# Delta-rule attention before two MoE layers: Gram tiles split by ScalarE and GpSimd, the unit diagonal by an identity product, block inverses spread with a full mask, norms of several groups at once

## The chip, the cores and the metric

One core of a Trainium2 chip. The metric is the device time of one execution, in microseconds, here as the median of three runs. Engines in the text: TensorE (PE, with PEld for its weight loads), VectorE (DVE), ScalarE (ACT), GpSimd (POOL) and SyncE (SP, which issues most DMAs).

## What is computed

The attention is a delta rule: per batch and head a 48x48 state is read and corrected at each of 768 steps. Two mixture-of-experts layers follow; the first is dense here, the second routes each token to one of eight experts.

```python
# q, k, v: [4, 8, 768, 48]; beta: [4, 8, 768]
k_n = k / (np.linalg.norm(k, axis=-1, keepdims=True) + 1e-06)
for t in range(S):
    y[:, :, t] = einsum('bhd,bhde->bhe', q[:, :, t], state)
    v_old = einsum('bhde,bhd->bhe', state, kt)
    state = state + bt * einsum('bhd,bhe->bhde', kt, vt - v_old)
x = y as [3072, 384]
x = leaky_relu(x @ w_in) @ w_out                 # d_ff 2048
out = x + gate * (relu(x @ w1[e]) @ w2[e])       # e: argmax of 8, only where x @ w_skip > 0
```

## The kernel before

The 768 steps are cut into six chunks of 128, the four batches into two pairs: twelve groups `i`, each one chunk of two batches of eight heads. Numbers are kept as a pair of f16 tiles, high and low part, so most products are two or three matmuls.

For a group, stage by stage: `prep` splits k and q into f16 parts and writes them to DRAM; `load_k`, `load_q` fetch them in the layouts that the products need. `norms` (L171) takes the squared norms of 128 tokens and 16 batch-heads on ScalarE and VectorE, an inverse square root by three Newton steps, and leaves four scales in the tile `dd`. `gram` (L221) is called four times per batch (`x` = 0 for k with k, `x` = 1 for k with q; `q` = 0, 1 for four heads each): 8 to 12 matmuls into PSUM, four ScalarE scalings into `g32` (L244), a GpSimd select that keeps the strict upper triangle (L245), for `x` = 0 past the first group a second one that writes 1 on the diagonal (L248), then VectorE makes the high part `gh` (L251) and the low part `gl` (L252). The buffers `g32` are two in rotation. The first group (`("hl", 0) in k`) gets its diagonal later, on the f16 tile, at L893.

`image` writes `gh` to DRAM, `sub16` reads its 16x16 diagonal blocks back and inverts them on VectorE (L273, L275), and `blocks` (L285) reads these inverses as `zc` and spreads them into block-diagonal 128x128 tiles `z128` on VectorE and `x128` on GpSimd (both L296), by a product with the mask `m8`, which is [128, 8] and repeated over the innermost 16 elements. `inv` builds the inverse of the whole triangle from the blocks: `pp` (L313) needs `x128`, `px` (L320), `pz` (L326); between rounds L329 restores the identity in parts of the tile `pe` on GpSimd, from the f32 identity. `solve` (L347) takes the chunk through: `ks`, `u0`, a first residual `r1` with `gh` and `gl`, `d1`, a second residual `r2`, `d2`, the state update `su` and the output `y`. `product` (L362) issues the matmuls of one of them, eight heads with 48 columns each.

The first MoE layer of a group (`m_up`, `m_down`, L753 to L785) starts when its group's `solve` is done and fills TensorE between the attention's products. Its two weight matrices are narrowed from 64-bit patterns by three VectorE operations per tile (L579 to L581), 32 tiles, early in the run: no `inv` but the first before 24 are in, no `solve` but the first before all 32 are. The second MoE layer follows after the attention.

The order of emission is written out by hand in `start()` for the first group and its loads; then a planner (`emit`) runs the stages as threads, with gates between them and due times from the table `T`. The tile framework orders each engine's instructions by a simulated timeline and by the priorities given there. Engines run their own instructions in order, so one that waits holds those behind it. Neither `T` nor the gates change.

Of the kernel before, what the change touches and what calls it, by code (L numbers as in the profile page):

```python
# [48 lines left out]
class Attention:  # L49
# [4 lines left out]
    def __init__(self, ctx, tc, kq, ktok, vtok, bet, ident):  # L54
# [15 lines left out]
        def mask(n, step, end, start):  # L70
# [13 lines left out]
        self.m8 = cp.tile([128, 8], F16, name="m_8")  # L84
        nc.vector.memset(self.m8, 1.0)
        nc.gpsimd.affine_select(out=self.m8, in_=self.m8, pattern=[[-16, 8]], compare_op=ALU.is_ge, fill=0.0,
                                base=0, channel_multiplier=1)
        nc.gpsimd.affine_select(out=self.m8, in_=self.m8, pattern=[[16, 8]], compare_op=ALU.is_ge, fill=0.0,
                                base=15, channel_multiplier=-1)
        self.pe = [cp.tile([128, H, C], F16, name=f"pe{i}") for i in range(2)]  # L90
# [80 lines left out]
    def norms(self, c, b0):  # L171
        nc = self.nc
        kt = self.ktile(c, b0)
        N = 2 * H
        be = self.p1.tile([128, N], F32, tag="be", name="be")
        nc.sync.dma_start(out=be, in_=self.bet[c * C:(c + 1) * C, b0 * H:(b0 + 2) * H])
# [3 lines left out]
        small = lambda nm: self.p1.tile([128, N], F32, tag=nm, name=nm)  # L180
        ss, y, t, nrm, d = (small(x) for x in ("ss", "y0", "t1", "nrm", "dd"))
        nc.vector.tensor_reduce(out=ss, in_=sq.rearrange("p b (h d) -> p (b h) d", d=D), axis=AX.X, op=ALU.add)
# [9 lines left out]
        nc.vector.tensor_scalar_add(out=nrm, in0=t, scalar1=1e-6)  # L192
        nc.vector.tensor_tensor(out=d, in0=nrm, in1=nrm, op=ALU.mult)
        nc.vector.reciprocal(out=d, in_=d)
        nc.vector.tensor_tensor(out=d, in0=d, in1=be, op=ALU.mult)
        dd = self.p4.tile([128, 4, N], F32, tag="d4", name="d4")
        for x, (src, f) in enumerate(((d, 2.0 ** -16), (d, 2.0 ** -8), (d, 256.0), (nrm, 256.0))):
            self.last = (nc.gpsimd if c + b0 else nc.vector).tensor_scalar(out=dd[:, x], in0=src, scalar1=f, scalar2=None, op0=ALU.mult)
        for j in range(2):
            self.tk[c, b0 + j]["dd"] = dd[:, :, j * H:(j + 1) * H]  # L200
# [20 lines left out]
    def gram(self, c, b, x, q, tag="g"):  # L221
# [63 lines left out]
    def blocks(self, c, b0):  # L285
# [6 lines left out]
        for j in range(2):  # L292
            k = self.tk[c, b0 + j]
            for x, nm in enumerate(("z128", "x128")):
                t = k[nm] = (self.p4 if x == 0 else self.p2).tile([128, H, C], F16, tag=nm, name=nm)
                (nc.gpsimd if x else nc.vector).tensor_tensor(out=t.rearrange("p h (g w) -> p h g w", w=16),  # L296
                                        in0=zc[:, x, j * H:(j + 1) * H].unsqueeze(2).to_broadcast([128, H, 8, 16]),
                                        in1=self.m8.unsqueeze(1).unsqueeze(3).to_broadcast([128, H, 8, 16]), op=ALU.mult)

    def inv(self, c, b):  # L300
# [7 lines left out]
        for n, m in ((16, self.m16), (32, self.m32)):  # L308
# [16 lines left out]
            for h in range(H):  # L325
# [3 lines left out]
            nc.gpsimd.tensor_copy(out=pe.rearrange("p h (g w) -> p h g w", w=64)[:, :, :, ws],  # L329
                                  in_=self.ident.rearrange("p (g w) -> p g w", w=64)[:, :, ws].unsqueeze(1).to_broadcast([128, H, 2, 16]))  # L330
# [16 lines left out]
    def solve(self, c, b):  # L347
# [14 lines left out]
        def product(nm, terms):  # L362
# [978 lines left out]
```

## Time and profile before

| | |
|---|---|
| median of 3 runs | 1164.93 us (1161.44 to 1170.25) |
| the profiled execution | 1159.18 us, of which its span is 1157.4 us |
| TensorE busy | 891.7 us, 77% |
| VectorE busy | 819.5 us, 71% |
| ScalarE busy | 617.4 us, 53% |
| GpSimd busy | 530.1 us, 46% |

Three stretches: to about 214 us the start, with the weight narrowing and the first group; to about 864 us the other eleven groups of attention with the first MoE layer in between; from there the last part of the first MoE layer and the second. The page's chain of waits covers only the last few microseconds before the end, so the stretches are read by the busy time of each engine in them and by what TensorE waited for. Busy time counts an instruction from its start to its end on the engine, also where it is held up on the way; overlapped matmuls count once.

### The profile page before, as it was taken

How to read it: one execution, taken by the hardware profiler on the slowest of the kernel's cores; microseconds unless marked ns; L12 is line 12 of the kernel's file. 1: busy time of each engine (PE TensorE's matmuls, PEld its weight loads, DVE VectorE, ACT ScalarE, POOL GpSimd, SP SyncE). 2: the span in 40 equal slices, each digit the busy share in tenths (PEclk: the TensorE clock that was granted, in tenths of full speed). 3: DMA queues.
4: the chain of work that ended last, by engine and by line, in shares of the span. 5: the costliest groups of instructions: out<-in, count | busy, mean ns of one | idle time of the engine just before them, and what ended most of it. 6: DMA issues, size and time to landing. Idle time of an engine off the chain costs nothing. (4 is left out here: it accounts for less than half of the span.)

```text
span 1157.4 us, 26616 instructions
## 1 busy us (share of the span) xinstructions
PE 891.7 (77%) x10164; PEld 680.7 (59%) x10164; DVE 819.5 (71%) x1814; ACT 617.4 (53%) x1406; POOL 530.1 (46%) x575
## 2 busy tenths in 40 slices
PE   2056778278886987778788979979987949998995
PEld 1056556265764766557566757667766637675763
DVE  6999998495986787566878575593447737777761
ACT  4476666255754755456355637464526425565540
POOL 4575685375455447364466544443224114332111
PEclk9999987678988898989989998999887979998998
DMA  7834775444454444354443212120108447788740
GB/s 206 227 89 135 226 181 124 83 141 85 127 96 105 110 103 107 37 124 76 126 106 66 70 21 70 25 65 15 43 28 230 127 144 256 258 281 265 234 149 16
DMA packets 201618, 144.03 MB, mean 124 GB/s; under 512 B 115070, under 2 KB 183892, under 8 KB 201482
## 3 DMA queue, kind: packets, MB, share of 16 engines
q1 hardware_dynamic: 189168, 123.24, 40.8%
q10 hardware_dynamic: 8570, 10.76, 3.3%
q0 software_dynamic: 3744, 8.27, 2.2%
q8 instruction: 81, 1.33, 0.5%
q14 instruction: 55, 0.45, 0.2%
HBM read 111.91 MB, written 30.92 MB: 123 GB/s over the span
## 5 line engine op out<-in xcount | busy, mean ns | idle before, releaser
L771 POOL TENSOR_TENSOR gll<-gg,ghh 128x512 f16<-128x512 f32 x96 | 119.0, 1242 | 99.1 <-ACT ghh L769 89.1
L761 PEld LDWEIGHTS <-wih 128*128 128x128 f16 x1152 | 118.9, 107 | 41.8 <-issue 18.1
L784 PE MATMUL o<-wol,ghh 128*128 128x394 f16 (+2 forms) x416 | 132.9, 325 | 8.0 <-DVE wol L608 8.0
L783 PE MATMUL o<-woh,ghh 128*128 128x394 f16 (+2 forms) x416 | 132.7, 329 | 4.7 <-ACT ghh L769 4.7
L244 ACT ACTIVATE g<-g,d 128x128 f32<-128x128 f32 x384 | 110.4, 376 | 41.4 <-DVE gl L252 23.8
L785 PE MATMUL o<-woh,gll 128*128 128x394 f16 (+2 forms) x416 | 124.3, 329 | 6.5 <-POOL gll L771 6.4
L761 PE MATMUL ph<-xh,wih 128*128 128x256 f16 x576 | 109.2, 302 | 12.8 <-ACT gg L766 10.6
L767 DVE SCALAR_TENSOR_TENSOR gg<-gg 128x512 f32<-128x512 f32 x96 | 83.4, 869 | 43.7 <-ACT gg L766 43.6
L761 PE MATMUL ph<-xl,wih 128*128 128x256 f16 x576 | 108.1, 299 | 2.3 <-DVE xl L691 2.3
L761 PE MATMUL ph<-xh,wil 128*128 128x256 f16 x576 | 108.2, 296 | 0.0
L245 POOL TENSOR_SCALAR_AFFINE_SELECT g<-g 128x512 f32<-128x512 f32 x96 | 72.8, 758 | 77.1 <-ACT g L244 67.6
L769 ACT CAST ghh<-gg 128x512 f16<-128x512 f32 x96 | 59.8, 623 | 83.3 <-DVE gg L767 83.0
L766 ACT COPY gg<-ph 128x512 f32<-128x512 f32 x96 | 56.4, 587 | 62.0 <-PE ph L761 52.4
L251 DVE CAST gh<-g 128x512 f16<-128x512 f32 x96 | 66.6, 696 | 30.0 <-POOL g L245 26.5
L1208 POOL DMA_INDIRECT out_dram<-y,ix x24 | 27.1, 1131 | 118.2 <-DVE y L1206 105.7
L252 DVE TENSOR_TENSOR gl<-g,gh 128x512 f16<-128x512 f32 x96 | 80.2, 836 | 0.7
L428 DVE SCALAR_TENSOR_TENSOR w1l<-ws,w1h 128x768 f16<-128x768 f32 x60 | 59.0, 996 | 27.6 <-ACT w1h L427 25.7
L273 DVE TENSOR_TENSOR tmp<-bt,z 128x15 f32<-128x15 f16 (+4 forms) x180 | 56.8, 316 | 29.5 <-DMA bt<-ai 19.6
L427 ACT ACTIVATE w1h<-ws 128x768 f16<-128x768 f32 x60 | 49.8, 840 | 39.0 <-DMA ws<-in_moe_w_dram 24.6
L296 POOL TENSOR_TENSOR x<-zc,m 128x1024 f16<-128x1024 f16 x24 | 56.5, 2372 | 29.3 <-DMA zc<-im 29.3
L1177 PEld LDWEIGHTS <-w1h 128*128 128x128 f16 x720 | 58.4, 99 | 19.2 <-issue 7.7
L747 POOL DMA_INDIRECT lst<-ids_i,pi x24 | 27.3, 1138 | 89.8 <-DMA lst<-ids_i,pi 45.6
(267 smaller groups left out, 2743.3 us busy)
## 6 DMA issues: line engine op xcount, KB each, us to landing
ws<-in_moe_w_dram SPq DMA_DIRECT2D x120, 384.0 KB
kt<-in_ktok_dram SPq DMA_DIRECT2D x24, 384.0 KB
x<-in_kq_dram SPq DMA_DIRECT2D x22, 384.0 KB
sc<-hl SPq DMA_DIRECT2D x22, 384.0 KB
raw<-in_moe_w_out_dram ACTq DMA_DIRECT2D x16, 384.0 KB
ai<-gh SPq DMA_DIRECT2D x24, 256.0 KB
x2s<-xs SPq DMA_DIRECT2D x24, 192.5 KB
vs<-in_vtok_dram SPq DMA_DIRECT2D x24, 192.0 KB
```

What stands on the lines that cost most here:

```text
L244: nc.scalar.activation(out=g32[:, j], in_=g[:, j], func=AF.Copy, scale=k["dd"][:, x, h:h + 1])
L245: nc.gpsimd.affine_select(out=g32, in_=g32, pattern=[[0, 4], [1, C]], compare_op=ALU.is_gt, fill=0.0, base=0, channel_multiplier=-1)
L251: self.last = nc.vector.tensor_copy(out=gh[:, hs], in_=g32)
L252: nc.vector.tensor_tensor(out=gl[:, hs], in0=g32, in1=gh[:, hs], op=ALU.subtract)
L428: nc.vector.scalar_tensor_tensor(out=lo, in0=src, scalar=scale, in1=hi, op0=ALU.mult, op1=ALU.subtract)
L761: nc.tensor.matmul(ph[:, j], lhsT=wt[:, d, fs], rhs=xx[:, d], start=(n == 0), stop=(n == 3 * KD - 1))
L767: nc.vector.scalar_tensor_tensor(out=g, in0=g, scalar=0.01, in1=g, op0=ALU.mult, op1=ALU.max)
L769: nc.scalar.copy(out=gh, in_=g)
L771: nc.gpsimd.tensor_tensor(out=gl, in0=g, in1=gh, op=ALU.subtract)
L783: nc.tensor.matmul(o, lhsT=gh[:, j, ts], rhs=wo[0][:, f, cols], start=(f == 0), stop=False)
L784: nc.tensor.matmul(o, lhsT=gh[:, j, ts], rhs=wo[1][:, f, cols], start=False, stop=False)
L785: nc.tensor.matmul(o, lhsT=gl[:, j, ts], rhs=wo[0][:, f, cols], start=False, stop=(f == NF1 - 1))
```

## The change

Five edits. (1) In `gram`, for all but the first group, the high part is a ScalarE copy and the low part a GpSimd subtraction; VectorE made both. The second select is gone, and L893 too. (2) `solve` gets the unit diagonal by one more matmul, of a 128x128 f16 identity with all eight heads at once (384 columns), ahead of `r1` and of `r2`. (3) `m8` is [128, 8, 16], so that the mask is read with unit step, and `x128` is made on VectorE like `z128`. (4) L329 runs on VectorE, from the f16 identity. (5) `norms` takes several groups: 0 and 1 alone, 2 and 3 together, 4 to 7, 8 to 11; loads, squares and reductions stay one per group, the chain of small operations after them is run once for all. Its `be` load now comes ahead of the first `kt` load.

```diff
-        self.m8 = cp.tile([128, 8], F16, name="m_8")
+        self.m8 = cp.tile([128, 8, 16], F16, name="m_8")
...
+        self.id16 = cp.tile([128, 128], F16, name="id16")
+        nc.vector.tensor_copy(out=self.id16, in_=ident)
...
-    def norms(self, c, b0):
+    def norms(self, groups):
         nc = self.nc
-        kt = self.ktile(c, b0)
-        N = 2 * H
...
-        yield 0, T["nl"]
-        sq = self.pl.tile([128, 2, HD], F32, tag="ld", name="sq")
-        nc.scalar.activation(out=sq, in_=kt, func=AF.Square)
...
+        n, (c0, b0) = len(groups), groups[0]
+        N = 2 * H * n
+        small = lambda nm: self.p1.tile([128, 8 * H], F32, tag=nm, name=nm)[:, 0:N]
...
+        for i, (c, b) in enumerate(groups):
+            kt = self.ktile(c, b)
+            yield 0, T["nl"]
+            sq = self.pl.tile([128, 2, HD], F32, tag="ld", name="sq")
+            nc.scalar.activation(out=sq, in_=kt, func=AF.Square)
+            nc.vector.tensor_reduce(out=ss[:, 2 * H * i:2 * H * (i + 1)], in_=sq.rearrange("p b (h d) -> p (b h) d", d=D),
+                                    axis=AX.X, op=ALU.add)
...
-        if x == 0 and not ("hl", 0) in k:
-            nc.gpsimd.affine_select(out=g32, in_=g32, pattern=[[0, 4], [1, C]], compare_op=ALU.not_equal,
-                                    fill=1.0, base=0, channel_multiplier=-1)
         hs = slice(4 * q, 4 * q + 4)
-        self.last = nc.vector.tensor_copy(out=gh[:, hs], in_=g32)
-        nc.vector.tensor_tensor(out=gl[:, hs], in0=g32, in1=gh[:, hs], op=ALU.subtract)
+        if ("hl", 0) in k:
+            self.last = nc.vector.tensor_copy(out=gh[:, hs], in_=g32)
+            nc.vector.tensor_tensor(out=gl[:, hs], in0=g32, in1=gh[:, hs], op=ALU.subtract)
+        else:
+            nc.scalar.copy(out=gh[:, hs], in_=g32)
+            nc.gpsimd.tensor_tensor(out=gl[:, hs], in0=g32, in1=gh[:, hs], op=ALU.subtract)
...
-                (nc.gpsimd if x else nc.vector).tensor_tensor(out=t.rearrange("p h (g w) -> p h g w", w=16),
+                nc.vector.tensor_tensor(out=t.rearrange("p h (g w) -> p h g w", w=16),
                                         in0=zc[:, x, j * H:(j + 1) * H].unsqueeze(2).to_broadcast([128, H, 8, 16]),
-                                        in1=self.m8.unsqueeze(1).unsqueeze(3).to_broadcast([128, H, 8, 16]), op=ALU.mult)
+                                        in1=self.m8.unsqueeze(1).to_broadcast([128, H, 8, 16]), op=ALU.mult)
...
-            nc.gpsimd.tensor_copy(out=pe.rearrange("p h (g w) -> p h g w", w=64)[:, :, :, ws],
-                                  in_=self.ident.rearrange("p (g w) -> p g w", w=64)[:, :, ws].unsqueeze(1).to_broadcast([128, H, 2, 16]))
+            nc.vector.tensor_copy(out=pe.rearrange("p h (g w) -> p h g w", w=64)[:, :, :, ws],
+                                  in_=self.id16.rearrange("p (g w) -> p g w", w=64)[:, :, ws].unsqueeze(1).to_broadcast([128, H, 2, 16]))
...
-        def product(nm, terms):
+        def product(nm, terms, plus=None):
             p = self.ps.tile([128, H, D], F32, tag=f"s{b % 2}", name=nm)
+            if plus is not None:
+                nc.tensor.matmul(p, lhsT=self.id16, rhs=plus, start=True, stop=False)
...
-        p = product("r1", [(of(ah), uh), (of(al), uh)])
+        p = product("r1", [(of(ah), uh), (of(al), uh)], uh)
...
-        p = product("r2", [(of(ah), ul)])
+        p = product("r2", [(of(ah), ul)], ul)
...
+    together = {0: 1, 1: 1, 2: 2, 4: 4, 8: 4}
+
     def stage_n(i):
-        c, p = groups[i]
-        yield from att.norms(c, 2 * p)
+        if i in together:
+            yield from att.norms([(c, 2 * p) for c, p in groups[i:i + together[i]]])
...
-        for b in range(2):
-            g = att.tk[0, b]["g", 0][0]
-            nc.gpsimd.affine_select(out=g, in_=g, pattern=[[0, H], [1, C]], compare_op=ALU.not_equal,
-                                    fill=1.0, base=0, channel_multiplier=-1)
```

## Rows read from the trace of the kernel before

**Rows 1.** Profile page: the span, and busy time of each engine

```profile
span 1157.4 us, 26616 instructions
...
PE 891.7 (77%) x10164; PEld 680.7 (59%) x10164; DVE 819.5 (71%) x1814; ACT 617.4 (53%) x1406; POOL 530.1 (46%) x575
```

**Rows 2.** Busy time of each engine in two stretches (stretch, its length, then by engine)

```profile
core 0: us, PE busy (x) PEld busy (x) DVE busy (x) ACT busy (x) POOL busy (x), PEclk, DMA share, GB/s
40.00:200.00 160.00, 106.62 (x1075) 86.25 (x1075) 150.08 (x313) 100.50 (x265) 108.53 (x113) 0.91 0.58 156
214.00:864.00 650.00, 525.09 (x6776) 404.44 (x6776) 441.53 (x1040) 348.37 (x853) 326.05 (x364) 0.90 0.35 80
```

**Rows 3.** Waits of TensorE, 214 to 864 us: total, times, longest

```profile
PE pp L313 <- POOL x L296: 41.9, 15, 16.8
PE y L366 <- DVE gh L251: 15.9, 7, 5.4
PE pz L326 <- DVE x L322: 12.2, 8, 3.9
PE d L366 <- ACT r L388: 9.5, 2, 7.3
PE ph L761 <- ACT gg L766: 6.4, 5, 3.1
```

**Rows 4.** VectorE's groups of instructions, 0 to 215 us: busy, mean ns of one

```profile
L252 DVE TENSOR_TENSOR gl<-g,gh 128x512 f16<-128x512 f32 x26 | 20.8, 803 | 0.0
...
L251 DVE CAST gh<-g 128x512 f16<-128x512 f32 x26 | 17.0, 660 | 1.7 <-POOL g L245 1.7
...
L190 DVE SCALAR_TENSOR_TENSOR y<-t,y 128x16 f32<-128x16 f32 x15 | 5.5, 365 | 0.1
...
L188 DVE TENSOR_TENSOR t<-y 128x16 f32<-128x16 f32 x15 | 4.9, 328 | 0.1
```

**Rows 5.** Groups of instructions by shape, whole span: busy, mean ns of one

```profile
L771 POOL TENSOR_TENSOR gll<-gg,ghh 128x512 f16<-128x512 f32 x96 | 119.0, 1242 | 99.1 <-ACT ghh L769 89.1 <-issue 6.5 <-PE o L785 3.3
...
L245 POOL TENSOR_SCALAR_AFFINE_SELECT g<-g 128x512 f32<-128x512 f32 x96 | 72.8, 758 | 77.1 <-ACT g L244 67.6 <-DVE sm L715 3.2 <-DVE tmp L273 3.1
...
L251 DVE CAST gh<-g 128x512 f16<-128x512 f32 x96 | 66.6, 696 | 30.0 <-POOL g L245 26.5 <-POOL g L248 3.4
...
L769 ACT CAST ghh<-gg 128x512 f16<-128x512 f32 x96 | 59.8, 623 | 83.3 <-DVE gg L767 83.0
...
L296 POOL TENSOR_TENSOR x<-zc,m 128x1024 f16<-128x1024 f16 x24 | 56.5, 2372 | 29.3 <-DMA zc<-im 29.3
...
L248 POOL TENSOR_SCALAR_AFFINE_SELECT g<-g 128x512 f32<-128x512 f32 x44 | 34.7, 788 | 1.6
...
L296 DVE TENSOR_TENSOR z<-zc,m 128x1024 f16<-128x1024 f16 x24 | 32.1, 1379 | 29.2 <-DMA zc<-im 29.0
...
L329 POOL CAST pe<-ident 128x256 f16<-128x256 f32 x48 | 24.7, 522 | 29.1 <-PE pz L326 22.2 <-ACT xs L795 5.5 <-ACT r L418 1.4
...
L356 DVE COPY shl<-sl 96x384 f16<-96x384 f16 x20 | 6.1, 313 | 1.1 <-PE y L366 1.1
```

**Rows 6.** Timeline, 365 to 372.5 us (start, duration, engine, line, operation, wait before)

```profile
365.30 2.36 DVE L296 TENSOR_TENSOR z<-zc,m 128x1024 f16<-128x1024 f16 x2 [6.85 <-DMA zc<-im]
...
366.48 5.24 POOL L296 TENSOR_TENSOR x<-zc,m 128x1024 f16<-128x1024 f16 x2 [4.76 <-DMA zc<-im]
...
369.47 0.59 PE L313 MATMUL pp<-x,gh 128*128 128x64 f16 x8 [5.15 <-POOL x L296]
```

**Rows 7.** Timeline, 310 to 311.5 us, GpSimd beside VectorE

```profile
310.17 0.83 POOL L217 TENSOR_TENSOR vs<-vs,d 128x384 f32<-128x384 f32 x1 [2.36 <-DVE y L190]
...
310.18 0.84 DVE L188 TENSOR_TENSOR t<-y 128x16 f32<-128x16 f32 x1
```

**Rows 8.** Timeline, TensorE, consecutive matmuls of 384 columns

```profile
1011.00 0.33 PE L1195 MATMUL o<-w2h,gh 128*64 128x384 f16 x1
1011.16 0.33 PE L1196 MATMUL o<-w2l,gh 128*64 128x384 f16 x1
```

More of the change, by code (lines that the diff above doesn't have):

```diff
@@ L169, in ktile @@
         return kt
-    def norms(self, c, b0):
+    def norms(self, groups):
         nc = self.nc
-        kt = self.ktile(c, b0)
-        N = 2 * H
-        be = self.p1.tile([128, N], F32, tag="be", name="be")
-        nc.sync.dma_start(out=be, in_=self.bet[c * C:(c + 1) * C, b0 * H:(b0 + 2) * H])
-        yield 0, T["nl"]
-        sq = self.pl.tile([128, 2, HD], F32, tag="ld", name="sq")
-        nc.scalar.activation(out=sq, in_=kt, func=AF.Square)
-        small = lambda nm: self.p1.tile([128, N], F32, tag=nm, name=nm)
-        ss, y, t, nrm, d = (small(x) for x in ("ss", "y0", "t1", "nrm", "dd"))
-        nc.vector.tensor_reduce(out=ss, in_=sq.rearrange("p b (h d) -> p (b h) d", d=D), axis=AX.X, op=ALU.add)
+        n, (c0, b0) = len(groups), groups[0]
+        N = 2 * H * n
+        small = lambda nm: self.p1.tile([128, 8 * H], F32, tag=nm, name=nm)[:, 0:N]
+        be, ss, y, t, d = (small(x) for x in ("be", "ss", "y0", "t1", "dd"))
+        if n == 1:
+            nc.sync.dma_start(out=be, in_=self.bet[c0 * C:(c0 + 1) * C, b0 * H:(b0 + 2) * H])
+        else:
+            nc.sync.dma_start(out=be.rearrange("p (c e) -> p c e", c=n // 2),
+                              in_=self.bet[c0 * C:(c0 + n // 2) * C, :].rearrange("(c t) e -> t c e", t=C))
+        for i, (c, b) in enumerate(groups):
[5 more added lines that the diff above has]
+                                    axis=AX.X, op=ALU.add)
         yi = y.bitcast(I32)
@@ L191, in norms @@
         nc.vector.tensor_tensor(out=t, in0=ss, in1=y, op=ALU.mult)
-        nc.vector.tensor_scalar_add(out=nrm, in0=t, scalar1=1e-6)
-        nc.vector.tensor_tensor(out=d, in0=nrm, in1=nrm, op=ALU.mult)
+        nc.vector.tensor_scalar_add(out=t, in0=t, scalar1=1e-6)
+        nc.vector.tensor_tensor(out=d, in0=t, in1=t, op=ALU.mult)
         nc.vector.reciprocal(out=d, in_=d)
         nc.vector.tensor_tensor(out=d, in0=d, in1=be, op=ALU.mult)
[L196 to L200, printed above, removed]
+        dd = self.pl.tile([128, 4, 8 * H], F32, tag="d4", name="d4")
+        for x, (src, f) in enumerate(((d, 2.0 ** -16), (d, 2.0 ** -8), (d, 256.0), (t, 256.0))):
+            self.last = (nc.gpsimd if c0 + b0 else nc.vector).tensor_scalar(out=dd[:, x, 0:N], in0=src, scalar1=f, scalar2=None, op0=ALU.mult)
+        for i, (c, b) in enumerate(groups):
+            for j in range(2):
+                self.tk[c, b + j]["dd"] = dd[:, :, (2 * i + j) * H:(2 * i + j + 1) * H]
     def scaled(self, c, b0):
@@ L360, in solve @@
         sb = lambda nm, dt: self.p2.tile([128, H, D], dt, tag=nm, name=nm)
-        def product(nm, terms):
+        def product(nm, terms, plus=None):
             p = self.ps.tile([128, H, D], F32, tag=f"s{b % 2}", name=nm)
+            if plus is not None:
+                nc.tensor.matmul(p, lhsT=self.id16, rhs=plus, start=True, stop=False)
             for h in range(H):
                 for i, (l, r) in enumerate(terms):
-                    nc.tensor.matmul(p[:, h], lhsT=l(h), rhs=r[:, h], start=(i == 0), stop=(i == len(terms) - 1))
+                    nc.tensor.matmul(p[:, h], lhsT=l(h), rhs=r[:, h], start=(plus is None and i == 0),
+                                     stop=(i == len(terms) - 1 and (plus is None or h == H - 1)))
             return p
@@ L861, in start @@
         after = lambda x: tc.issue_after(x.ins)
-        nm, ks = att.norms(0, 0), [att.first(b, 0) for b in range(2)]
+        nm, ks = att.norms([(0, 0)]), [att.first(b, 0) for b in range(2)]
         for g in [nm] + ks:
```

5 lines of the change are left out of this document (3 added, 2 removed).

## The prediction

> **What bounds the kernel now.** First the page: over the span no engine is full, TensorE 77%, VectorE 71%, ScalarE 53%, GpSimd 46% [rows 1]. That is an average over unlike stages, so next the busy time by stretch. Between 40 and 200 us VectorE works 150.1 of 160 us, TensorE 106.6: the start runs at VectorE's pace. Between 214 and 864 us TensorE works 525.1 of 650 us at a granted clock of 0.90, VectorE 441.5, ScalarE 348.4, GpSimd 326.1 [rows 2]. There TensorE is the nearest to full, and the attention's chain puts 125 us of holes into it. The rest of the span, after 864 us, holds no instruction of the change, and I take it as moved whole.
>
> The third view is what ended TensorE's waits in the long stretch. One line leads: `pp` waits for `x128` from GpSimd, 41.9 us in 15 waits. Then `y` for `gh` with 15.9, `pz` for VectorE's addition to `x` with 12.2, a residual's cast with 9.5, `ph` for a ScalarE copy with 6.4 [rows 3]. So what the change moves stands ahead of 57.8 of the 125 us; the others are ordinary hand-overs that a less loaded VectorE may serve sooner.
>
> **The change part by part.**
>
> *Gram halves.* Of 96 gram tiles, eight (two batches, `x` = 0 and 1, two halves) stay as they are, 88 move. VectorE loses a cast and a subtraction each; in the start, where 26 of the 96 run, they cost 0.66 and 0.80 us [rows 4]. That is 18 x 1.46 = 26.3 us of VectorE there, and 70 x about 1.5 = 105 us in the long stretch. ScalarE gains 88 casts; the same shape, f32 to f16, 128x512, costs it 0.62 us in the first MoE layer [rows 5], 11 us in the start and 44 in the long stretch, which makes its 348 there 392 of 650. GpSimd gains 88 subtractions; L771 is the same operation on the same shape at 1.24 us [rows 5], so 109 us in all. It loses 44 second selects at 0.79, 24 spreads at 2.37 and 48 restorations at 0.52, 116 us [rows 5], and the two of L893. GpSimd ends about level.
>
> A rule of the Trainium skill speaks against this part: the page GPSIMD Engine Reference, section 4.1 Engine selection, sends two-input elementwise work to VectorE and calls GpSimd about twice as slow. By that rule one of them would take about 1.67 us, an estimate, 0.43 more than the row; if every `r1` after the first group waited for its last low half, 22 x 0.43 would add 9 us to the sum below, 1139. The row is on the very shape, and the sum goes by it.
>
> Each high part comes after one select where `x` = 0 had two, so `gh` is ready 0.8 us earlier, and its low part about 0.4 us later than with VectorE. Behind a ScalarE cast that waits for its select stand the casts of `solve`, the scalings of `inv` and the MoE copies, all in one queue; this is the second rival.
>
> *Spreading `x128`.* At 365 to 370 us the wait can be read: `zc` lands in two parts, `z` starts at 365.30, `x` at 366.48; GpSimd needs 5.24 us for its two tiles, and `pp` starts at 369.47, 5.15 us idle before it [rows 6]. After the change VectorE makes z, x, z, x. No row shows this product with a unit-step mask, so its price is bounded: above by today's `z` at 1.38 us, below by the f16 copy L356 at 0.31 for 384 elements, 0.83 for 1024 at that rate [rows 5]. I take 0.83, because L356 is the only row whose operands are all f16 in SBUF with unit step, as all three are after the change; what bars this today is the mask repeated over the innermost elements. Then the first `x` is done at 366.48 + 0.83 = 367.3 instead of about 369.4, 2.1 us sooner; at 1.38 each it is 368.1, 1.3 sooner. VectorE's own bill is 48 x 0.83 - 24 x 1.38 = +7 us (+33 with 1.38).
>
> The page VectorE: DVE Perf Modes of the Trainium skill, section The perf-mode tier table, gives a two-input operation with all operands 16-bit in SBUF twice the rate; its figures make 0.69 us here, an estimate. With that VectorE would pay 48 x 0.69 - 33 = 0, and the time would be a microsecond or two lower.
>
> *Restoring `pe`.* 48 copies of 256 elements, at L356's 0.31 [rows 5] some 15 us on VectorE. I cost them at nothing on the path: no wait of [rows 3] hangs on them, and VectorE's 208 idle us of the long stretch [rows 2] cover their share there; without that cover it is up to 13 us. The start's share is in its sum.
>
> *Norms.* Two lines of the chain, six of its sixteen operations, cost 5.5 + 4.9 us in five calls of the start [rows 4], so a chain is about (10.4 / 5) x 16/6 = 5.5 us. Five chains replace twelve: VectorE saves 7 x 5.5 = 39 us, less perhaps 5 for the wider rows. In the start it is one chain (the fifth of today's five), and it pulls the squares and reductions of groups 5 to 7 forward. I set this to zero there. The loads of `kt` for later groups move ahead on SP's queue, past the loads of the groups between; 384 KB each, at a DMA share of 0.35 in the long stretch [rows 2] I cost that at nothing. Without that cover a load of k or q would come late and `gram` with it. `be` ahead of the first `kt` costs one issue, about half a microsecond, on the way to the first gram.
>
> *Identity products.* 48 matmuls of 384 columns. Consecutive ones of that width start 0.16 us apart [rows 8]: 44 in the long stretch are +7.0 us on TensorE, whole, because TensorE is nearest to full there.
>
> **The sum.** Start: VectorE loses 26.3 and gains about 4 (eight copies at 0.31, and four x at 0.83 less what its four z save), so 22 of 150 us. It doesn't all become time, since the loader also passes through ScalarE, GpSimd and DMA; bounds are 0 and 22, I take half: -11. Long stretch: `pp` waits, 2.1 us off the longest and about 1.3 off each of the other fourteen, whose mean is 1.8: -20. `y` waits for `gh`: half of 15.9, -8. The waits for VectorE's other results (12.2, and the 9.5 behind VectorE's residual): VectorE falls from 441 to about 441 - 105 - 30 + 19 = 325, a quarter; a quarter of 21.7 is -5. ScalarE is 13% fuller: +3 on what waits for it. Identity: +7. Together -23. Nothing is counted for the clock, though it may rise if holes go. All in all -34, from the profiled execution's own 1159.2 to 1125. The median of the runs stands 5.7 above that execution, so on its scale I predict 1130 us, 3.0% faster.
>
> **Rivals.**
>
> (a) *The holes move.* `pp` waits less for the spread and then `px` or `pz` waits for the next ScalarE or VectorE step, and only the start and the sharpest waits gain: -11, a third of the -33 in the long stretch, +3 and +7, or -12, 1153 us. For it: in the long stretch 125 us of holes have many causes [rows 3], and the change leaves most of these alone. Against it: the leading two causes are what is moved.
>
> (b) *ScalarE's queue stalls, slower.* VectorE now waits 26.5 us for L245 before casts [rows 5]; after the change ScalarE does. If the order lets it wait out the whole select, 0.76 us [rows 5], at 70 tiles, that is 53 us on the engine that also feeds every step of `solve` and `inv`. ScalarE would then be at 445 of 650 us; if all 53 reach TensorE, the long stretch stands at -23 + 53 = +30 and with the start's -11 the kernel at +19, 1184 us. It decides for slower from 34 us of such stalls on. Against it: VectorE, fuller than ScalarE, wasted half of that in the same place.
>
> (c) *GpSimd holds VectorE.* A VectorE operation with two SBUF inputs, 16 elements wide, took 0.84 us beside a GpSimd product of 0.83 [rows 7], where the same line's mean is 0.33 [rows 4]. The page GPSIMD Engine Reference, section 8 Key points, says as much: the two share their SBUF interfaces. GpSimd has 109 us of two-input work more and 57 (the spreads) less; if the selects and copies that it loses never held VectorE, 52 us of new holding meet a VectorE busy half the time, 26 us of the 130 that it is relieved of. A fifth of the gains that hang on VectorE (11, 8 and 5) is 5 us: 1135.
>
> (d) *The spread stays slow.* With 1.38 us VectorE pays 26 us more, 10 of it on `pp`: 14 x 0.5 + 0.8 is 8 us, and 2 in the start: 1140.
>
> **Chances.** Forecast with (c) and (d) as its variants 0.58 (1115 to 1145 as its own range), (a) 0.24, (b) 0.12, a start that gains all 22 us together with a higher clock in the long stretch 0.06, near 1100. A difference under 1% can hardly be told from no change here. Faster by over 1% (below 1153): 0.58 + 0.06 + half of (a) = 0.76; within 1%: the other half of (a), 0.12; slower: (b), 0.12. The range from 1098 to 1160 takes in the forecast, the good case and most of (a).
>
> **What would show it.** `pp` (L313) waiting for VectorE's L296 with well under 42 us; L296 twice as often at 0.7 to 0.9 us; VectorE between 40 and 200 us below 135 and the last tile of the weight narrowing some 10 us earlier; `gh` by ScalarE at about 0.62 us and `gl` by GpSimd at 1.24; five runs of the norms' chain; 48 wide matmuls. The prediction is wrong if the list of TensorE's waits is led by ScalarE's `gh` or by anything behind it, if VectorE's busy time falls by over 100 us and the holes of 125 us stay, or if the stretch after 864 us changes its length.

## The result, and the profile after

The changed kernel takes 1126.5 us (median of four runs, 1119.6 to 1129.4) where the kernel before takes 1164.0 beside it: a ratio of 0.966, with a 95% interval from 0.960 to 0.972. The profiled execution took 1127.6 us. The prediction of 1130 us holds. Its sum does not: several of its terms are wrong in ways that cancel, and the runs below take them one by one.

The page of after, its span and busy times, the answer to [rows 1]:

```profile
span 1125.8 us, 26420 instructions
PE 881.0 (78%) x10212; PEld 679.8 (60%) x10212; DVE 724.2 (64%) x1599; ACT 658.6 (58%) x1494; POOL 500.9 (44%) x517
```

VectorE lost 95 us, ScalarE gained 41, GpSimd lost 29. TensorE, with 48 matmuls more, is busy 11 us less. So the work was moved as the diff says; whether that made the time is another question.

Busy time by stretch of after, with the columns of [rows 2]; the first row is the one that answers there. The others cut the span where the output of the second group's `solve` has been copied into `xh`, the tile that feeds the first MoE layer (221 us), where the last group's has been, which is called the attention's end here (793), and where the first MoE layer ends (881):

```profile
40.00:200.00 160.00, 110.43 (x1119) 89.24 (x1119) 136.38 (x297) 111.51 (x284) 93.44 (x98) 0.87 0.63 169
...
0.00:221.00 221.00, 124.50 (x1299) 101.95 (x1300) 174.10 (x396) 139.84 (x346) 121.66 (x144) 0.86 0.67 174
221.00:793.00 572.00, 481.43 (x6579) 377.84 (x6578) 352.38 (x814) 364.87 (x902) 290.18 (x303) 0.91 0.38 83
793.00:881.00 88.00, 72.84 (x611) 52.90 (x610) 41.08 (x114) 36.22 (x62) 29.32 (x25) 0.92 0.37 103
881.00:1126.00 245.00, 202.22 (x1730) 147.12 (x1728) 156.69 (x278) 117.63 (x188) 59.70 (x47) 0.93 0.63 201
```

The same cuts of before (214, 864 and 924 us); the long stretch between them is the second row of [rows 2]:

```profile
0.00:214.00 214.00, 121.86 (x1320) 99.42 (x1321) 189.63 (x430) 129.97 (x328) 131.45 (x152) 0.93 0.62 165
...
864.00:924.00 60.00, 51.81 (x417) 37.47 (x417) 44.30 (x95) 31.36 (x52) 17.89 (x14) 0.85 0.62 172
924.00:1157.00 233.00, 192.97 (x1655) 139.35 (x1652) 144.09 (x251) 107.73 (x174) 54.66 (x45) 0.93 0.62 199
```

Length less TensorE's busy time is its idle time, so the two fences give the whole balance (us, after minus before):

```
stretch                          length   TensorE busy   TensorE idle
start, to the 2nd group's solve      +7            +3             +4
the other groups' attention         -78           -44            -34
rest of the first MoE layer         +28           +21             +7
second MoE layer                    +12            +9             +3
sum                                 -31           -11            -20
```

This table is the main reading. The attention ends 71 us earlier (the 7 us of the longer start are already in that), and 40 of these come back behind it: 28 in the rest of the first MoE layer, with 21 us more of TensorE work, and 12 in the second layer. Part of the 12 is only the cut: before, 54 of the second layer's 1080 up products (L1177), 6.6 us of TensorE, ran ahead of it, and after none (L1188). What is truly gone is 20 us of holes and 11 us of busy time. By its last `y` the attention is done even 86 us earlier (862.5 and 776.7 us); why 16 of these are lost before `xh` is written is told under the question of TensorE's work.

TensorE's waits from 214 to 793 us of after, the answer to [rows 3]:

```profile
PE pp L324 <- DVE x L307: 28.3, 12, 8.8
PE g L251 <- DMA qd<-sc: 9.0, 4, 5.4
PE y L379 <- DVE S L425: 6.5, 3, 5.9
PE g L251 <- ACT g L254: 6.4, 4, 4.3
PE pz L337 <- DVE x L333: 6.4, 4, 4.5
```

The spread still leads with 28.3 us (41.9 before), now from VectorE. The wait of `y` for `gh` (15.9) is all but gone, the one of `pz` is halved. What the operations cost, whole span, the answer to [rows 5]:

```profile
L263 POOL TENSOR_TENSOR gl<-g,gh 128x512 f16<-128x512 f32 x88 | 107.5, 1226 | 45.3 <-ACT gh L262 42.0 <-DVE x L333 2.9
L262 ACT CAST gh<-g 128x512 f16<-128x512 f32 x88 | 55.4, 633 | 35.7 <-POOL g L255 35.3 <-PE y L379 0.2
L307 DVE TENSOR_TENSOR z<-zc,m 128x1024 f16<-128x1024 f16 x24 | 26.3, 1129 | 31.3 <-DMA zc<-im 31.3
L307 DVE TENSOR_TENSOR x<-zc,m 128x1024 f16<-128x1024 f16 x24 | 24.4, 1046 | 2.0 <-PE pp L346 1.7 <-DMA zc<-im 0.2
L340 DVE COPY pe<-id 128x256 f16<-128x256 f16 x48 | 16.8, 362 | 8.8 <-PE pz L337 8.8
L376 PE MATMUL r<-uh,id 128*128 128x384 f16 x24 | 8.4, 362 | 4.7 <-ACT uh L397 4.7
L376 PE MATMUL r<-ul,id 128*128 128x384 f16 x24 | 7.8, 351 | 1.6 <-ACT ul L407 1.6
```

### The profile page after: what moved, and what is told of

It is laid out like the page before. It is cut to its first block, busy times and chain, and to the rows that moved or that the text cites. A ratio compares the mean times of both kernels' runs of the same rounds, so it can differ in the third digit from the quotient of the medians.

```text
span 1125.8 us, 26420 instructions
## 1 busy us (share of the span) xinstructions
PE 881.0 (78%) x10212; PEld 679.8 (60%) x10212; DVE 724.2 (64%) x1599; ACT 658.6 (58%) x1494; POOL 500.9 (44%) x517
## 5 line engine op out<-in xcount | busy, mean ns | idle before, releaser
L787 POOL TENSOR_TENSOR gll<-gg,ghh 128x512 f16<-128x512 f32 x96 | 114.4, 1194 | 133.7 <-ACT ghh L785 125.3
L783 DVE SCALAR_TENSOR_TENSOR gg<-gg 128x512 f32<-128x512 f32 x96 | 83.2, 868 | 97.6 <-ACT gg L782 97.2
L777 PEld LDWEIGHTS <-wih 128*128 128x128 f16 x1152 | 115.7, 103 | 34.2 <-issue 11.9
L263 POOL TENSOR_TENSOR gl<-g,gh 128x512 f16<-128x512 f32 x88 | 107.5, 1226 | 45.3 <-ACT gh L262 42.0
L777 PE MATMUL ph<-xh,wih 128*128 128x256 f16 x576 | 103.2, 288 | 8.2 <-ACT gg L782 4.1
L255 POOL TENSOR_SCALAR_AFFINE_SELECT g<-g 128x512 f32<-128x512 f32 x96 | 69.3, 722 | 82.7 <-ACT g L254 75.4
L777 PE MATMUL ph<-xh,wil 128*128 128x256 f16 x576 | 102.7, 283 | 0.0
L777 PE MATMUL ph<-xl,wih 128*128 128x256 f16 x576 | 101.4, 286 | 1.1 <-DVE xl L707 1.1
L262 ACT CAST gh<-g 128x512 f16<-128x512 f32 x88 | 55.4, 633 | 35.7 <-POOL g L255 35.3
L1188 PEld LDWEIGHTS <-w1h 128*128 128x128 f16 x720 | 59.1, 100 | 17.3 <-issue 5.5
L1165 POOL DMA_INDIRECT xg<-x2s,ix x24 | 35.6, 1484 | 68.6 <-DMA ix<-lst 48.6
L1206 PE MATMUL o<-w2h,gh 128*128 128x384 f16 (+1 forms) x192 | 63.4, 330 | 1.3 <-ACT gh L1192 1.3
```

What stands on the lines that cost most here:

```text
L263: nc.gpsimd.tensor_tensor(out=gl[:, hs], in0=g32, in1=gh[:, hs], op=ALU.subtract)
L777: nc.tensor.matmul(ph[:, j], lhsT=wt[:, d, fs], rhs=xx[:, d], start=(n == 0), stop=(n == 3 * KD - 1))
L783: nc.vector.scalar_tensor_tensor(out=g, in0=g, scalar=0.01, in1=g, op0=ALU.mult, op1=ALU.max)
L787: nc.gpsimd.tensor_tensor(out=gl, in0=g, in1=gh, op=ALU.subtract)
L1188: nc.tensor.matmul(ph[:, j], lhsT=wt[:, d, fs], rhs=xx[:, d], start=(n == 0), stop=(n == 3 * KD - 1))
L1206: nc.tensor.matmul(o, lhsT=gh[:, j, ts], rhs=wh[:, f], start=(f == 0), stop=False)
```

## The experiments

Two questions were open after this. Which edit brings the gain: the theory of the prediction gives most of it to the spread (20 us) and to the gram halves (24 us: 11 in the start, 8 and 5 behind it), nothing to norms and to `pe`. And what is left over: the theory takes TensorE for the engine nearest to full, a rival holds that the gain is limited by something else. Kernels whose label begins with a are the changed kernel with one part undone or altered, those with b the kernel before with one part alone. Ratios are to the kernel before on the same chip, with 95% intervals.

**One part undone.** First the gram halves back on VectorE, with all else of the change kept (`a_halves_vector`):

```diff
-            nc.scalar.copy(out=gh[:, hs], in_=g32)
-            nc.gpsimd.tensor_tensor(out=gl[:, hs], in0=g32, in1=gh[:, hs], op=ALU.subtract)
+            nc.vector.tensor_copy(out=gh[:, hs], in_=g32)
+            nc.vector.tensor_tensor(out=gl[:, hs], in0=g32, in1=gh[:, hs], op=ALU.subtract)
```

> The kernel after, but all high and low parts of the Gram tiles are made by VectorE as before (one select, identity product kept). By the prediction's steps the start gives back 11 us and the long stretch 13 less 3: 1147. Rival: the halves only change engines, what counts is the spread and the missing select: 1126 to 1132.

Measured: 1119.4 us, 0.966 (0.959 to 0.972), the same ratio as the whole change. VectorE took 60 us of work back and the kernel lost nothing. Two views of this run say more. The spread's lines on VectorE, and TensorE's waits from 214 to 864 us:

```profile
L307 DVE TENSOR_TENSOR z<-zc,m 128x1024 f16<-128x1024 f16 x24 | 19.0, 830 | 10.2 <-DMA zc<-im 10.0
L307 DVE TENSOR_TENSOR x<-zc,m 128x1024 f16<-128x1024 f16 x24 | 17.6, 765 | 0.9 <-DMA zc<-im 0.9
```

```profile
PE o L799 <- ACT ghh L785: 16.1, 12, 3.5
PE ph L777 <- ACT gg L782: 11.4, 5, 4.6
PE ks L379 <- DVE xl L707: 10.2, 6, 6.8
...
PE pp L324 <- DVE x L307: 4.4, 7, 1.1
```

The same product takes 0.80 us on average here and 1.09 in the changed kernel, where GpSimd makes the low halves (0.90 in `b_spread` below, where VectorE makes them too): GpSimd's two-input work does hold VectorE up. And `pp` waits 4.4 us instead of 28.3, at the same time of the kernel. The length of that wait is no measure of what the kernel loses by it.

Then `x128` back on GpSimd, with the full mask (`a_spread_gpsimd`):

```diff
-                nc.vector.tensor_tensor(out=t.rearrange("p h (g w) -> p h g w", w=16),
+                (nc.gpsimd if x else nc.vector).tensor_tensor(out=t.rearrange("p h (g w) -> p h g w", w=16),
```

> The kernel after, but x128 is spread by GpSimd again, with the full mask. By the prediction's step the wait of pp grows by 1.3 us at each of 15 places, 20 us: 1146. Rival (the holes move): TensorE finds other work or waits for the next step, and no more than 5 to 8 us come back: 1131 to 1134.

Measured: 1127.9 us, 0.974 (0.967 to 0.981). That is 0.8% above the change, some 9 us by the ratios, with intervals that overlap. With the other edits in, `x128`'s place is worth less than half of the 20 us that the prediction gave it, if it is worth anything. The wait at which I had read the price, TensorE from 214 to 864 us:

```profile
PE pp L324 <- POOL x L307: 4.5, 7, 1.1
```

Even with GpSimd at 2.17 us a tile (the median), `pp` hardly waits.

The second select and L893 back, the identity products out (`a_diag_select`):

```diff
+        if x == 0 and not ("hl", 0) in k:
+            nc.gpsimd.affine_select(out=g32, in_=g32, pattern=[[0, 4], [1, C]], compare_op=ALU.not_equal,
+                                    fill=1.0, base=0, channel_multiplier=-1)
...
-        p = product("r1", [(of(ah), uh), (of(al), uh)], uh)
+        p = product("r1", [(of(ah), uh), (of(al), uh)])
...
-        p = product("r2", [(of(ah), ul)], ul)
+        p = product("r2", [(of(ah), ul)])
...
```

> The kernel after, but the diagonal is written by the second GpSimd select and L893 again, without the identity products. By the prediction's step 48 wide matmuls leave TensorE, 7 us, and the select's 0.8 us ahead of gh costs less than that: 1119 to 1126. Rival: 35 us more on GpSimd, which now also makes the low parts, and the later gh cost more than the matmuls: 1132 to 1140.

Measured: 1124.7 us, 0.969 (0.962 to 0.975): no difference from the change. TensorE's busy time falls from 881.0 to 874.0, the 7 us that the identity products were costed at, and the kernel gets nothing for them.

The norms one group at a time (`a_norms_single`):

```diff
-        dd = self.pl.tile([128, 4, 8 * H], F32, tag="d4", name="d4")
+        dd = self.p4.tile([128, 4, 2 * H], F32, tag="d4", name="d4")
...
-    together = {0: 1, 1: 1, 2: 2, 4: 4, 8: 4}
+    together = {i: 1 for i in range(12)}
```

> The kernel after, but the norms of one group at a time, as before. The prediction's steps put the joint norms at nothing on the path: 1126 us, within 5. First rival: the four joint loads ahead of group 4 keep the DMA queue and the buffers that the loads of group 1 and 2 need at 195 to 225 us, and the gap of TensorE there closes: 1116 to 1120. Second rival: the 39 us of VectorE that the joint chain saves are worth a third of themselves: 1135 to 1140.

Measured: 1121.5 us, 0.965 (0.959 to 0.972). Worth nothing. The price of the chain was right: its small operations (L194 to L207) take 64.2 us of VectorE here and 27.6 in the changed kernel, 36.6 less where 39 less 5 were worked out (L197 runs 36 times at 0.35 us here; there six times each at 0.24 us on 16 elements and 0.56 on 64, three times at 0.19 on 32). Yet VectorE's busy time differs by only 4 us (728 against 724): other instructions take longer in the changed kernel, the spread's products (L307) by 9 us and the first MoE layer's L783 by 7. A saving on an engine need not show in its busy time.

So of the four parts undone one by one, only the spread's place is perhaps missed. That asks for the other direction.

**One part alone.** The spread, both mask and place (`b_spread`):

```diff
-        self.m8 = cp.tile([128, 8], F16, name="m_8")
+        self.m8 = cp.tile([128, 8, 16], F16, name="m_8")
...
-                (nc.gpsimd if x else nc.vector).tensor_tensor(out=t.rearrange("p h (g w) -> p h g w", w=16),
+                nc.vector.tensor_tensor(out=t.rearrange("p h (g w) -> p h g w", w=16),
...
-                                        in1=self.m8.unsqueeze(1).unsqueeze(3).to_broadcast([128, H, 8, 16]), op=ALU.mult)
+                                        in1=self.m8.unsqueeze(1).to_broadcast([128, H, 8, 16]), op=ALU.mult)
```

> The kernel before with the full mask and x128 on VectorE alone. Taking single edits out of the kernel after moved it by -1 to +7 us (spread: +7), so two accounts remain. Additive: an edit alone gives what it takes back when left out, here 7 us: 1153 where before is 1160. Saturating: once the attention is somewhat quicker, TensorE's own work and the stretch behind the attention set the time, and each larger edit alone reaches most of the 39 us: 1130 or less. The prediction's step (20 us on pp): 1140.

Measured: 1116.8 us, 0.964 (0.961 to 0.968). This edit alone brings as much as all five together, 41 us and twice its term. The line of its `x128`, and the first of TensorE's waits from 214 to 864 us:

```profile
L296 DVE TENSOR_TENSOR x<-zc,m x24: 677/685/1642, 56.1 to 685.7; 128x1024 f16<-128x1024 f16 x24
```

```profile
PE pp L313 <- DVE x L296: 22.8, 14, 6.1
PE o L785 <- POOL gll L771: 16.4, 9, 3.1
PE o L783 <- ACT ghh L769: 11.1, 11, 2.4
```

(The first row gives least, median and greatest duration in ns, then the first and the last start.) Here, too, `pp` waits on, and the time is gone all the same.

The spread's two halves: the place alone, with the narrow mask (`b_x_narrow`), and the full mask alone, with `x128` on GpSimd (`b_mask_only`):

```diff
-                (nc.gpsimd if x else nc.vector).tensor_tensor(out=t.rearrange("p h (g w) -> p h g w", w=16),
+                nc.vector.tensor_tensor(out=t.rearrange("p h (g w) -> p h g w", w=16),
```

> The kernel before with x128 moved to VectorE, the narrow mask kept: each of the two tiles at about 1.4 us instead of 0.69. The full mask with the move gave 39 us of the kernel before, 1117 where before is 1158. If the unit step is what counts (x128 sooner), most of it goes: 1145 or more. If it is GpSimd's queue, freed of 2.3 us at a time, that counts: 1118 to 1125. The prediction's own step: 8 to 10 us of it, 1127.

```diff
-        self.m8 = cp.tile([128, 8], F16, name="m_8")
+        self.m8 = cp.tile([128, 8, 16], F16, name="m_8")
...
-                                        in1=self.m8.unsqueeze(1).unsqueeze(3).to_broadcast([128, H, 8, 16]), op=ALU.mult)
+                                        in1=self.m8.unsqueeze(1).to_broadcast([128, H, 8, 16]), op=ALU.mult)
```

> The kernel before with the full mask, x128 still by GpSimd. z128 on VectorE gets down to about 0.69 us; x128 is late as before. If the time hangs on when x128 is there and on GpSimd's queue: 1153 to 1160, unless GpSimd's product gets quicker too. If VectorE's relief counts (24 x 0.69 = 17 us): 1145.

Measured: the place alone 1131.9 us, 0.976 (0.971 to 0.981); the mask alone 1141.4, 0.982 (0.976 to 0.988). Together 2.4% and 1.8% are 4.2%, and both at once gave 3.6%: here the parts nearly add. The first time lies between the two accounts put up for it, the second below both of its own, so neither the earlier `x128` nor GpSimd's queue nor VectorE's relief is the whole of it. The product's row in the two runs, as above, first the place alone, then the mask alone:

```profile
L296 DVE TENSOR_TENSOR x<-zc,m x24: 1209/1217/2177, 56.6 to 756.2; 128x1024 f16<-128x1024 f16 x24
```

```profile
L296 DVE TENSOR_TENSOR z<-zc,m x24: 679/688/973, 53.4 to 708.4; 128x1024 f16<-128x1024 f16 x24
L296 POOL TENSOR_TENSOR x<-zc,m x24: 2105/2153/2916, 55.5 to 711.4; 128x1024 f16<-128x1024 f16 x24
```

On VectorE the unit step takes the product from 1.22 to 0.69 us; on GpSimd only from 2.34 (the median before) to 2.15.

The halves alone (`b_halves`):

```diff
-        self.last = nc.vector.tensor_copy(out=gh[:, hs], in_=g32)
-        nc.vector.tensor_tensor(out=gl[:, hs], in0=g32, in1=gh[:, hs], op=ALU.subtract)
+        if ("hl", 0) in k:
+            self.last = nc.vector.tensor_copy(out=gh[:, hs], in_=g32)
+            nc.vector.tensor_tensor(out=gl[:, hs], in0=g32, in1=gh[:, hs], op=ALU.subtract)
+        else:
+            nc.scalar.copy(out=gh[:, hs], in_=g32)
+            nc.gpsimd.tensor_tensor(out=gl[:, hs], in0=g32, in1=gh[:, hs], op=ALU.subtract)
```

> The kernel before with the high and low parts of the Gram tiles on ScalarE and GpSimd alone, second select kept. Additive: 1160 (left out it gave back nothing). Saturating: 1130 to 1138. The prediction's steps (24 us): 1136. GpSimd would be at 57% with nothing taken off it, so a loss is possible too: 1165.

Measured: 1162.7 us, 1.002 (0.999 to 1.006): nothing. Its waits and its busy times from 214 to 864 us:

```profile
PE g L241 <- ACT g L244: 16.4, 9, 5.2
PE d L370 <- DVE r L401: 12.5, 5, 4.4
PE ph L765 <- ACT gg L770: 11.0, 5, 5.7
...
PE pp L317 <- POOL x L300: 6.7, 7, 2.0
```

```profile
214.00:864.00 650.00, 532.22 (x6665) 406.19 (x6663) 416.10 (x867) 382.28 (x928) 398.32 (x437) 0.89 0.35 78
```

This is rival (a) in pure form. The wait of `pp` fell from 41.9 to 6.7 us without the spread being touched, since the order around it moved, and the holes stayed (650 less 532 is 118 us idle, 125 before): others wait instead, `g` for its ScalarE scalings first. GpSimd went from 326 to 398 us of the 650, since without the other edits it gains the subtractions and loses nothing.

The identity products with the selects gone (`b_identity`: edit 2 of the change and the removed selects of edit 1) and the restoration of `pe` on VectorE (`b_pe_vector`: edit 4), each alone:

```diff
...
-            nc.gpsimd.tensor_copy(out=pe.rearrange("p h (g w) -> p h g w", w=64)[:, :, :, ws],
-                                  in_=self.ident.rearrange("p (g w) -> p g w", w=64)[:, :, ws].unsqueeze(1).to_broadcast([128, H, 2, 16]))
+            nc.vector.tensor_copy(out=pe.rearrange("p h (g w) -> p h g w", w=64)[:, :, :, ws],
+                                  in_=self.id16.rearrange("p (g w) -> p g w", w=64)[:, :, ws].unsqueeze(1).to_broadcast([128, H, 2, 16]))
```

> The kernel before with the restoration of pe on VectorE from the f16 identity alone. Additive: this edit would have to carry the rest of the 39 us that the four others (7 + 0 + 4 + 0) don't, 1132. Saturating, and the prediction's step (nothing on the path): 1155 to 1160.

```diff
...
-        if x == 0 and not ("hl", 0) in k:
-            nc.gpsimd.affine_select(out=g32, in_=g32, pattern=[[0, 4], [1, C]], compare_op=ALU.not_equal,
-                                    fill=1.0, base=0, channel_multiplier=-1)
...
+            if plus is not None:
+                nc.tensor.matmul(p, lhsT=self.id16, rhs=plus, start=True, stop=False)
...
```

> The kernel before with the identity products in place of the diagonal's selects alone. Additive: 4 us, 1156. Saturating: 1135 to 1145, by gh 0.8 us sooner. The prediction's step: 7 us more on TensorE, 1160 to 1167.

Measured: `pe` 1147.0 us, 0.991 (0.988 to 0.994); identity 1134.5, 0.983 (0.978 to 0.989). Both shortened the kernel before; I had given the first nothing and the second +7 us. (The first gain is no larger than what two builds may differ by, as is said at the end.) These two and the spread all take work off GpSimd: 3.6%, 1.7% and 0.9%, 6.2% together, of which the whole change shows 3.4%. That GpSimd's load is the cause is not shown: the mask alone leaves it as it was (530 us busy before, 533 with it) and brings 1.8%.

**Is TensorE's work the floor?** Both kernels without the third of the three products of the first MoE layer's `m_up`:

```diff
-            for wt, xx in ((wih, xh), (wih, xl), (wil, xh)):
+            for wt, xx in ((wih, xh), (wih, xl)):
...
```

> The kernel after without the third product of the first MoE layer's up matmuls (low part of the weights): the output lacks this part. TensorE loses 576 matmuls of 256 columns that start 0.11 us apart, 63 us. If TensorE's own work sets the time of the kernel after (why single edits left out cost so little): 1126 - 55 to 63, 1063 to 1071. If the chain of the attention still does: 1095 or more.

> The kernel before without the third product of the first MoE layer's up matmuls: the output lacks this part. If the attention's chain holds back the kernel before, TensorE's 63 us come out by a half or less: 1125 to 1140, and the distance to the kernel after with the same cut grows to 60 us or more. If TensorE's work sets the time there as well: 1095 to 1103, and the distance stays at 39.

Measured: on the changed kernel 1112.7 us, 0.959 (0.954 to 0.964), 14 us below it (8 by the ratios); on the kernel before 1127.5, 0.971 (0.965 to 0.977), 33 us below it. Left out are 576 matmuls, 63 us at the 0.11 us from one to the next. TensorE's busy time falls by 38 us in the changed kernel (881 to 843 in the profiled executions) and by 50 in the kernel before (892 to 842). It falls by less than 63 at least in part because of the clock: TensorE is busy at the lower of its two granted levels for 171 us where the changed kernel had 131, and for 182 where the kernel before had 148. The kernel's time falls by 8 to 14 us and by 33, so with two products TensorE's own work sets the time of neither. The distance between the two kernels shrinks from 39 to 14 us by the ratios, where the expectations had 60 or more, or 39.

That does not show what holds the changed kernel with all three products, since the cut changes the limit. The tile `xh` has two buffers. In the changed kernel, from the seventh group on, each copy into it starts within 2.1 us of the last up product that reads the buffer it takes, and the first MoE layer turns to the group only 33 to 75 us later: there the attention waits for that layer and not the layer for the attention. The last group, after; `yt` are the transposes ahead of the copy:

```profile
778.51 0.82 PE L703 MATMUL yt<-ident,r 128*128 128x128 f32 x6
...
791.98 0.86 ACT L706 CAST xh<-yt 128x384 f16<-128x384 f32 x2 [1.95 <-PE ph L777]
```

In the kernel before, and in both kernels with two products, the buffer has been free for 23 us or more at every such copy from the third group on, and the layer starts at most 12 us behind it: there it waits for the attention. Before, the last group (`cnt` is TensorE's last instruction ahead of the copy and not read by it):

```profile
862.51 0.90 PE L687 MATMUL yt<-ident,r 128*128 128x128 f32 x3 [0.58 <-ACT r L418]
...
863.45 0.48 ACT L690 CAST xh<-yt 128x384 f16<-128x384 f32 x1 [0.99 <-PE cnt L1007]
...
863.98 0.80 PE L761 MATMUL ph<-xh,wih 128*128 128x256 f16 x3 [0.56 <-ACT xh L690]
```

So the change took the second half of the long stretch from the one limit to the other, and the cut of the third product took it back. No run has a third buffer of `xh`, which would test this.

## Why the prediction was right, and where its steps were wrong

The signs by which it was to be judged: 48 wide matmuls, `gh` at 0.63 us (0.62 foretold), `gl` at 1.23 (1.24), the spread 48 times on VectorE at a median of 0.69 for `x128` and 0.74 for `z128` (0.7 to 0.9; the mean, with hold-ups, is 1.09), five norm chains, VectorE between 40 and 200 us at 136.4 (below 135) and the weight narrowing's last third operation at 168 instead of 188 us: these came as foretold or nearly. One of the three conditions for its being wrong came, too: the stretches behind the attention changed their length.

**Start, -11.** Wrong: +7 by the copy into `xh`, +4 by the second group's last `y` (210.9 and 215.2 us). VectorE was relieved by 14 us between 40 and 200, the narrowing ended earlier, and the second group's `solve` ended later. The stretch around that end, after:

```profile
199.00:221.00 22.00, 8.99 (x146) 8.14 (x144) 11.38 (x25) 10.99 (x27) 12.14 (x13) 0.50 0.57 114
```

No engine is over 12.1 of 22 us busy, and the clock granted to TensorE is its lower level throughout (1.2 GHz, 0.50); before, the same 22 us show 0.73. The step that failed is that the start runs at VectorE's pace: a quicker VectorE brought the narrowing forward and not the `solve` behind it. Among the runs the end of that `solve` lies anywhere from 206 us (mask alone) to 231 (`pe` alone) without following VectorE's work; with the halves back on VectorE it is 208. What exactly delays it in the changed kernel stays open; of the last microseconds the trace shows that the transposes are done at 216.4 and that ScalarE, which waits 2.8 us for a load of `prep` (L119) in between, copies them from 220.5.

**`pp` waits, -20.** The edit was the right one, the size and the way of reading it wrong. Alone the spread brings 41 us, and beside the other edits its place brings some 9. Neither can be read from the list of waits: the kernels within 1% of each other have 4.4, 4.5, 10.6 (norms single), 28.3 and 31.0 us (second select) of waits for the spread, and `b_halves` took 35 us of them away for nothing. The wait's total says where TensorE stood, not what the spread's late end costs further down the chain.

The price of the product came out at 0.69 us, where I took 0.83, scaled up from a copy of 384 elements. Durations don't scale with the elements alone: at the least, the copy of 256 (L340) takes 0.21 us and the product of 1024 takes 0.68. The rule of the Trainium skill (VectorE: DVE Perf Modes, The perf-mode tier table) gives 0.69, an estimate from the table's times for 2048 elements, and the median of `x128` agrees with it to the hundredth.

**Gram halves, -8 and -5, and the rest of the start's gain.** Wrong: nothing, by both runs. VectorE fell from 71% to 64%, and relieving it in this way was worth nothing; that it was the busiest engine of the start misled me. The low half comes later by the new path (a cast on ScalarE, then 1.23 us on GpSimd), which may pay back what an earlier `gh` brings; the two were not separated. The -5 for VectorE's relief and the +3 for a fuller ScalarE were shares of waits that no row gave, and no run separates them either.

**Holes, -33 + 3.** The size is right, -34, but the gain was counted as the kernel's, and 28 us of first-MoE remainder came behind the attention. "Moved whole" failed: work that fills holes has to run somewhere when the holes go. Before, TensorE worked 52 us between the attention's end and that of this layer (6.6 of them for the second), after 73.

**Identity, +7.** Right as TensorE's time (881.0 against 874.0), wrong as the kernel's: undone in the changed kernel it gives nothing back, and put alone into the kernel before, with the selects gone, it brought 24 us instead of costing 7. That every microsecond of TensorE's work counts whole, "because TensorE is nearest to full", is the step that failed.

**Clock, 0.** It isn't zero, and it goes both ways. The granted clock fell in the start (0.93 to 0.86), stood almost still in the long stretch (0.90 to 0.91) and rose in the remainder (0.85 to 0.92). Worked out from the records of matmuls and of the clock, TensorE is busy at the lower of its levels for 148 us before and 131 after (start 27 and 43, long stretch 95 and 70, behind it 27 and 18). A product of `m_up` follows the one before it by 0.109 us at the upper level and by 0.213 at the lower (medians, before), so half of the 17 us less is the saving, -8, an estimate. With the +7 of identity, that leaves -10 of the measured -11 that I can't ascribe; matmuls that follow each other with fewer breaks overlap more, and overlapped time counts once, which would go that way but isn't shown.

**`pe` and norms, 0.** Norms: right, and the saving on VectorE, put at 39 less 5 us, too, at 36.6. `pe`: 0.9% alone; on top of the others it wasn't tried.

So the cause that led the sum, the spread, was the right one, and that the total came out within 4 us was luck: the spread, which alone is worth twice its term, and the clock, which had none, stood against two terms that failed (start, halves) and one that was not seen (the work behind the attention). No sum of measured terms gives the 37 us, since the gains of single edits don't add.

**The rivals.** (a), the holes move: not for the change as a whole, but exactly so for the halves alone. (b), ScalarE waits out the selects: ScalarE idles 35.3 us before its casts for L255, more than the 34 us named as the turning point, but TensorE's wait behind them is a few microseconds and the kernel with VectorE in that place is no faster. (c), GpSimd holds VectorE: shown as a mechanism, the mean of 1.09 us against 0.80 and 0.90 in the two kernels without the subtractions; 48 x 0.29 is at most 14 us of VectorE, and it costs the kernel nothing that can be told, since the halves' place is level. The timeline of after shows the worst places plainly (start, duration, engine, line, operation, wait before):

```profile
403.66 5.49 DVE L307 TENSOR_TENSOR z<-zc,m 128x1024 f16<-128x1024 f16 x2 [4.57 <-DMA zc<-im]
...
405.02 2.25 POOL L263 TENSOR_TENSOR gl<-g,gh 128x512 f16<-128x512 f32 x2
...
410.11 1.28 DVE L307 TENSOR_TENSOR x<-zc,m 128x1024 f16<-128x1024 f16 x2
...
410.84 0.59 PE L324 MATMUL pp<-x,gh 128*128 128x64 f16 x8 [8.84 <-DVE x L307]
```

Two products that take 1.4 us when left alone take 5.49 while GpSimd works, and `pp` waits 8.84. The page GPSIMD Engine Reference of the Trainium skill, section 8 Key points, says that the two share their SBUF interfaces; the trace agrees. The rule of the same page that GpSimd takes about twice VectorE's time (section 4.1) would have put the subtraction at an estimated 1.67 us; it took 1.23. (d), the spread stays slow: excluded by the rows, with medians of 0.69 and 0.74 us against the 1.38 that it supposed.

**What stays open.** What sets the common level of 1117 to 1128 us, at which the change, four of its altered forms and the spread alone all lie. VectorE's load doesn't (60 us more of it cost nothing), nor does the wait for the spread (4.4 to 31.0 us at one time). Why single gains don't add is answered in part: the spread alone and three of the altered forms hold the attention at `xh` from the seventh group on as the changed kernel does (within 5 us of the buffer), and there a quicker attention gains nothing. But the form with the halves on VectorE ends at the same level without that, and the identity, mask and `pe` edits alone show it at 1134 to 1147 us, so it isn't the whole answer. Whether TensorE's work sets the pace of the first MoE layer there is not shown; from 510 to 777 us TensorE is busy for 227 of 267 us. Each build's instructions are ordered anew, and orders differ far beyond the edited lines, so that differences of about 1% between two builds can't be put down to the edit with certainty. The spread alone, with five lines changed, does as well as all five edits; no run with the whole output is clearly faster than it, and the changed kernel with the halves on VectorE is level.

## What to carry to other kernels

A broadcast over the innermost elements of one operand can cost a 16-bit product almost half its rate; look for such operands first, since spelling the operand out costs a little memory and, in these runs, no time (the mask alone 1.8% faster). Don't add up the waits of a list as gains: a wait that vanishes can come back under another name (41.9 to 6.7 us for nothing), and an edit can bring twice the wait that it takes away (41.9 to 22.8 us of wait, 41 us of time). When a stage has filler work in its holes, shortening the stage pushes the filler behind it, so count the stage's gain less what has to run afterwards. And look which side waits where one stage hands a buffer to the next: once the attention waits for its buffer, quickening it further is of no use.

## What the hardware showed beyond what was expected

- A product of two f16 operands, 128x1024 in SBUF: 0.69 us on VectorE with unit step throughout, 1.22 with one operand repeated over its innermost 16. On GpSimd the same step is worth 8%, 2.34 to 2.15 us (medians).
- VectorE's 0.69 us product reached 4.25 us (its greatest duration after, at 403.66 us) beside GpSimd's two-input work.
- A copy of 256 f16 elements takes 0.36 us on average on VectorE (median 0.22) beside 0.52 (median 0.40) for the cast from f32 on GpSimd that it replaces.
